# Attention and two gated layers on one core: the band mask added by TensorE in batches 0 and 1, and batch 1's band exponentials cut into 12 ScalarE pieces

## The chip, the cores and the metric

The kernel runs on one core of a Trainium2 chip. The metric is the device time of one execution in microseconds (us). The kernel before took 923.15 us, the median of three runs (922.99 to 925.22). The profiled execution is a run of its own and took 925.11 us.

## The reference, cut to what matters

Attention over 4 batches, 8 heads, 576 positions and 64 columns is computed twice: on positions averaged in fours (144 of them), and on a band in which each position sees only those less than 4 away. Both results are added, and two gated layers follow (512 to 1536 to 512, and 512 to 2048 to 512).

```
mask = np.abs(pos[:, None] - pos[None, :]) < factor          # factor = 4
scores = scale * np.matmul(q, k.transpose(0, 1, 3, 2))
scores = np.where(mask, scores, -1000000000.0)
scores = scores - np.max(scores, axis=-1, keepdims=True)
attn = np.exp(scores)
attn = attn / (np.sum(attn, axis=-1, keepdims=True) + 1e-09)
out_local = np.matmul(attn, v)
return (out_up + out_local).astype(np.float32)
```

The gated layers are `(sigmoid(x @ w_gate) * (x @ w_val)) @ w_out` and `(h * sigmoid(1.702 h)) @ w_out` with `h = x @ w_in`.

## The kernel before, in words

Attention is cut into 16 jobs (`class Job`): four batches, and in each four pairs of heads (`hp`). A job first pools its queries and keys in fours on GpSimd (`pool4`, tiles `half`, `qd`, `kd`). Its band is computed in 24 blocks of 24 queries by 30 keys (`NT`, `NQ`, `NU`): for each block and head one small TensorE matmul writes 32 x 30 scores into a PSUM tile `ss` of 128 partitions, in which the 24 blocks stand as 4 partition quarters by 6 groups (`NG`), for two heads: 2 x 180 columns (`scores`, L668). VectorE then adds the mask into the SBUF tile `sc` (L684), takes the maximum of each group of 30 (L694) and subtracts it (L695); ScalarE exponentiates all 360 columns at once (L697); VectorE sums (L698), inverts (L700), multiplies (L701) and transposes (L702). `band` (L785) multiplies the weights with the values on TensorE. The pooled attention goes beside it: scores (`pooled`, L710), maximum (L727), four exponentials on ScalarE that take the maximum as bias and give the row sum as a second output (L736), the inverse (L743, L744), scaling (L750), transposes (L770), a copy out of PSUM (`pdt`, L775) and the product (L807). The sum of both (`xf`, L820) is split into a high part (`xhi`, L831) and a remainder (`xlo`, L833).

The gated layers multiply in three passes of a high and a low part (L927 to L929); ScalarE makes the high part of each weight (L864) and VectorE the low part (L867). In layer 1 of batch 0 the weights also come as 64-bit words and are converted by ScalarE (L851) and VectorE (L853 to L857). Batch 0's attention has to be done before its layer 1 can begin; the attention of batches 1 to 3 is laid between the matmuls of layer 1 of the batch before. From the second job of batch 1 on, a job is `merged`: band scores and pooled scores share one PSUM tile, `pa`, the only double bank that is left then.

Each engine runs a fixed list of instructions. `class Plan` writes the lists: every operation is registered with `op(engine, nanoseconds, function, reads, writes, due)`, and `order` then places the operations one after another on the engine that is free first, by due time, with the costs that `op` was given. `BEGIN` says when each engine is taken to be free at the start. Where TensorE would be idle in the plan before layer 1 is in full run, fillers are placed: matmuls of the tile `warm` into an unused bank (L1420, 512 or 128 columns). At least one filler stands ahead of each small TensorE operation from 8 us on. A change of an operation or a cost anywhere moves the lists of all engines behind it.

Before the plan begins, `warm` is set to zero by VectorE (L469), GpSimd builds the fp32 mask (L483 to L493) and the fp32 identity `ident` for the transposes.

Of the kernel before, what the change touches and what calls it, by code (L numbers as in the profile page):

```python
# [10 lines left out]
F32 = mybir.dt.float32  # L11
BF16 = mybir.dt.bfloat16
# [3 lines left out]
AF = mybir.ActivationFunctionType  # L16
ALU = mybir.AluOpType
AX = mybir.AxisListType

P = 128  # L20
# [58 lines left out]
class Plan:  # L79
# [12 lines left out]
    MARGIN = 8.0e3  # L92
    WARM_FROM = 8.0e3
    WARM_LEAST = 1
    BEGIN = {"pe": 0.0, "act": 2000.0, "dve": 2200.0, "pool": 3900.0, "sp": 600.0}

    def __init__(self):
        self.ops = []
# [189 lines left out]
def tile_multiscale_attention_gated_ffn(  # L288
# [9 lines left out]
    nc = tc.nc  # L298
    B, NHP, _, S = qT.shape
    D = 64  # L300
# [8 lines left out]
    SCALE = 1.0 / 8.0  # L309
# [13 lines left out]
    NQ, NU = 24, 30  # L323
    NT = S // NQ
    NG = NT // 4
# [3 lines left out]
    sb = ctx.enter_context(tc.tile_pool(name="sb", bufs=1))  # L329
# [5 lines left out]
    op, buf = plan.op, plan.buf  # L335
# [114 lines left out]
    def bank(some):  # L450
        banked.append(Buf(None, some))
        return banked[-1]
# [13 lines left out]

    sb.tile([P, 72], F32, name="inset", tag="inset")
    warm = sb.tile([P, P], BF16, name="warm", tag="warm")
    nc.vector.memset(warm, 0.0)  # L469
    for s in [*qslots, *plan.rings["qt0"][0]]:  # L470
        nc.vector.memset(s.t[:, S:], 0.0)
    for s in [*kslots, *plan.rings["kt0"][0]]:
# [5 lines left out]
    for s in pslots:  # L478
        nc.vector.memset(s.t, 0.0)
        nc.vector.memset(s.t[:, :, :, NU:NU + 1], 1.0e-9)  # L480
    mask = sb.tile([P, NG, NU], F32, name="mask", tag="mask")
    band = plan.rings["xf"][0][0].t[:, :NU]
    nc.gpsimd.memset(band, 0.0)  # L483
    for i in range(4):
# [7 lines left out]
                            fill=NEG, base=-3, channel_multiplier=0)  # L492
    nc.gpsimd.affine_select(out=mask[96:, NG - 1], in_=mask[96:, NG - 1], pattern=[[-1, NU]],  # L493
                            compare_op=ALU.is_ge, fill=NEG, base=S + 2 - NQ * (NT - 1), channel_multiplier=0)
    ident = Buf(Slot(sb.tile([P, P], F32, name="ident", tag="ident")))
    op("pool", 650.0, lambda: make_identity(nc, ident.t), [], [ident], -10.0e3)


    def act_ns(n, psum=False):
        return (126.0 if psum else 190.0) + n / 1.2  # L500

    def dve_ns(n, two=False):
        return 69.0 + n / (1.92 if two else 0.96)
# [1 line left out]
    def pool_ns(n):  # L505
        return 140.0 + 2.12 * n

    def dma(out_, in_, nbytes, reads, writes, due, after=0.0):
        op("sp", nbytes, lambda: nc.sync.dma_start(out=out_, in_=in_), reads, writes, due, after)


    QUANTUM = 3 * 227.0
# [93 lines left out]
    class Job:  # L606
# [49 lines left out]
        def scores(self):  # L656

            ss = bank(self.banks)
            qt, kt, sc, pt, tt, nm, sm = self.qt, self.kt, self.sc, self.pt, self.tt, self.nm, self.sm
            n = NG * NU  # L660

            def scored():
                for t in range(NT):
                    g, i = divmod(t, 4)
                    t = NG * i + g
                    for h in range(2):
                        hs = slice(h * D, (h + 1) * D)
                        nc.tensor.matmul(ss.t[32 * i:32 * i + 32, h, g * NU:(g + 1) * NU],  # L668
                                         qt.t[hs, NQ * t:NQ * t + 32], kt.t[hs, NQ * t:NQ * t + NU],
                                         start=True, stop=True, tile_position=(h * D, 32 * i))  # L670

            when = self.due(0.1)
            if not self.merged:
                op("pe", 1500.0, scored, [qt, kt], [ss, sc], when)
            else:
                qd, kd, nmd, smd, pd = self.qd, self.kd, self.nmd, self.smd, self.pd

                def pe():
                    scored()
                    self.pooled(ss, n)  # L680

                op("pe", 1700.0, pe, [qt, kt, qd, kd],
                   [ss, sc, nmd, (smd, 0), (smd, 1), (pd, 0), (pd, 1)], when)
            op("dve", dve_ns(2 * n), lambda: nc.vector.tensor_add(  # L684
                sc.t.rearrange("p h g c -> p h (g c)"), ss.t[:, :, :n],
                mask.rearrange("p g c -> p (g c)")[:, None, :].to_broadcast([P, 2, n])), [ss], [sc], when)
            if self.merged:
                self.pooled_softmax(ss, n, when, [sc])
# [8 lines left out]
            op("act", act_ns(2 * n), lambda: nc.scalar.activation(p, sc.t, AF.Exp, scale=SCALE), [sc], [pt], at)  # L697
            op("dve", dve_ns(2 * n), lambda: nc.vector.reduce_sum(sm.t, pt.t[:, :, :, :NU + 1], axis=AX.X),  # L698
               [pt], [sm], at)
            op("dve", 155.0, lambda: nc.vector.reciprocal(sm.t, sm.t), [], [sm], at)  # L700
# [765 lines left out]
```

## Time and profile before

| what | value |
|---|---|
| median of three runs | 923.15 us |
| profiled execution | 925.11 us |
| its span | 923.4 us |
| outside the span | 1.7 us |
| TensorE (PE) busy | 909.3 us, 98% of the span |
| VectorE (DVE) busy | 757.0 us, 82% |
| ScalarE (ACT) busy | 508.3 us, 55% |
| GpSimd (POOL) busy | 80.8 us, 9% |

The profile page gives the busy time of each engine over the span. Other views of the trace are used below: busy time and granted TensorE clock by stretch, the waits of an engine, the chain of work that ended last (start, length, engine, tile, line), groups of instructions by line, and the timeline (start, length, engine, line, operation, tiles, shape, count, and the idle time before it with what ended it). Starts are us from the beginning of the span. `pa`, `acc` and `ph` are PSUM banks.

### The profile page before, as it was taken

What the parts mean: (1) busy time and instruction counts of PE and PEld (TensorE: products, weight loads), DVE (VectorE), ACT (ScalarE), POOL (GpSimd) and SP (SyncE); (2) the same over time, 40 slices, a digit from 0 to 9 for tenths busy, and PEclk for the clock granted to TensorE, in tenths of its full rate; (3) what the DMA queues carried; (4) which work ended last, traced back from release to release, by engine and by line L of the source; (5) the groups of instructions that cost most, each with busy time, mean ns of one, the idle gap of its engine ahead of it and who ended that gap; (6) DMA issues with size and microseconds to landing.
All of it is one profiled execution on the core that took longest, in us unless ns stands there. A gap on an engine that the chain in (4) does not pass through costs nothing.

```text
span 923.4 us, 18997 instructions
## 1 busy us (share of the span) xinstructions
PE 909.3 (98%) x7378; PEld 761.8 (83%) x7378; DVE 757.0 (82%) x1432; ACT 508.3 (55%) x1094; POOL 80.8 (9%) x123
## 2 busy tenths in 40 slices
PE   8999999999999999999999999999999999999997
PEld 4677787788888887889999998888888888888896
DVE  4899998988878888899999898878977887765474
ACT  3756664645555555565545655545664553554463
POOL 6211201111011100010000000000301100000000
PEclk8999999999999999999999999999999999999999
DMA  9448548365375834434311651102531100152101
GB/s 287 124 155 229 188 157 244 110 183 174 114 204 185 248 108 135 159 110 141 109 49 42 222 193 46 46 24 84 190 115 69 46 35 34 40 180 78 43 4 23
DMA packets 63949, 113.76 MB, mean 123 GB/s; under 512 B 8241, under 2 KB 29563, under 8 KB 63858
## 3 DMA queue, kind: packets, MB, share of 16 engines
q1 hardware_dynamic: 63858, 112.54, 39.2%
q8 instruction: 58, 0.95, 0.5%
q14 instruction: 33, 0.27, 0.1%
HBM read 82.37 MB, written 30.15 MB: 122 GB/s over the span
## 4 chain that ended last, share of the span: by engine, by line
PE 94%; DVE 2%; POOL 1%; DMA 1%; issue 1%; ACT 1%; POOLq 0%; ACTq 0%
PE ph L927 13%; PE ph L929 13%; PE ph L928 13%; PE acc L927 8%; PE acc L928 8%; PE acc L929 8%; PE pa L927 7%; PE pa L928 7%; PE pa L929 7%; PE pa L785 2%; PE pa L668 1%; PE pa L710 1%; PE pa L770 1%; PE pa L807 1%; PE acc L1420 1%
## 5 line engine op out<-in xcount | busy, mean ns | idle before, releaser
L864 ACT CAST whi<-w 128x512 fp32r<-128x512 f32 x151 | 92.4, 613 | 77.4 <-PE ph L929 28.3
L927 PE MATMUL ph<-xhi,whi 128*128 128x512 f32 (+1 forms) x322 | 127.6, 396 | 0.0
L929 PE MATMUL ph<-xlo,whi 128*128 128x512 f32 (+1 forms) x322 | 124.4, 386 | 0.0
L928 PE MATMUL ph<-xhi,wlo 128*128 128x512 f32 (+1 forms) x322 | 124.4, 386 | 0.0
L867 DVE TENSOR_TENSOR wlo<-w,whi 128x512 fp32r<-128x512 f32 x149 | 103.9, 699 | 17.5 <-ACT whi L864 17.3
L864 ACT CAST whi<-wr 128x512 fp32r<-128x512 f32 (+1 forms) x99 | 55.7, 565 | 35.9 <-PE acc L929 16.5
L867 DVE TENSOR_TENSOR wlo<-wr,whi 128x512 fp32r<-128x512 f32 (+1 forms) x99 | 62.2, 630 | 15.6 <-ACT whi L864 14.7
L927 PE MATMUL acc<-ghi,whi 128*128 128x512 f32 (+1 forms) x192 | 73.7, 384 | 0.0
L927 PEld LDWEIGHTS ph<-xhi,whi 128*128 128x128 f32 x322 | 60.9, 189 | 14.7 <-issue 1.6
L1041 DVE TENSOR_TENSOR w<-pa,w 128x512 f32<-128x512 f32 (+1 forms) x112 | 70.2, 627 | 3.3 <-PE pa L929 2.6
L928 PE MATMUL acc<-ghi,wlo 128*128 128x512 f32 (+1 forms) x192 | 72.4, 377 | 0.4 <-DVE wlo L867 0.4
L929 PE MATMUL acc<-glo,whi 128*128 128x512 f32 (+1 forms) x192 | 72.3, 377 | 0.5 <-DVE glo L867 0.5
L929 PEld LDWEIGHTS ph<-xlo,whi 128*128 128x128 f32 x322 | 60.8, 189 | 12.5
L928 PEld LDWEIGHTS ph<-xhi,wlo 128*128 128x128 f32 x322 | 61.0, 189 | 11.3
L927 PE MATMUL pa<-w,whi 128*128 128x512 f32 (+1 forms) x168 | 61.5, 366 | 0.1
L929 PE MATMUL pa<-w,whi 128*128 128x512 f32 (+1 forms) x168 | 61.4, 366 | 0.0
L928 PE MATMUL pa<-w,wlo 128*128 128x512 f32 (+1 forms) x168 | 61.4, 366 | 0.0
L864 ACT CAST w<-w 128x512 fp32r<-128x512 f32 x51 | 31.1, 619 | 35.7 <-PE pa L929 20.4
L867 DVE TENSOR_TENSOR w<-w,w 128x512 fp32r<-128x512 f32 x48 | 34.3, 721 | 17.0 <-ACT w L864 16.8
L961 ACT ACTIVATE th<-ph 128x512 f32<-128x512 f32 (+1 forms) x44 | 24.6, 559 | 42.8 <-PE ph L929 42.8
L927 PEld LDWEIGHTS acc<-ghi,whi 128*128 128x128 f32 x192 | 36.0, 188 | 7.4 <-issue 1.7
L966 DVE SCALAR_TENSOR_TENSOR th<-th,ph 128x512 f32<-128x512 f32 (+1 forms) x44 | 27.9, 634 | 17.1 <-PE ph L929 12.2
(286 smaller groups left out, 2307.0 us busy)
## 6 DMA issues: line engine op xcount, KB each, us to landing
w<-w SPq DMA_DIRECT2D x68, 512.0 KB
w2d<-we SPq DMA_DIRECT2D x32, 256.0 KB
w<-gd SPq DMA_DIRECT2D x32, 256.0 KB
gd<-w SPq DMA_DIRECT2D x30, 256.0 KB
st<-x2d SPq DMA_DIRECT2D x52, 128.0 KB
w<-w2d SPq DMA_DIRECT2D x16, 256.0 KB
wr<-w2d SPq DMA_DIRECT2D x16, 256.0 KB
out<-ev SPq DMA_DIRECT2D x16, 256.0 KB
```

Of the source, the lines that this page charges most:

```text
L668: nc.tensor.matmul(ss.t[32 * i:32 * i + 32, h, g * NU:(g + 1) * NU], qt.t[hs, NQ * t:NQ * t + 32], kt.t[hs, NQ * t:NQ * t + NU], start=Tru ...
L710: nc.tensor.matmul(ss.t[:GH, h, c + r * G:c + (r + 1) * G], qd.t[h * D:(h + 1) * D, r * GH:(r + 1) * GH], kd.t[h * D:(h + 1) * D, :], star ...
L770: nc.tensor.transpose(ss.t[:GH, h, o:o + GH], pd.t[:, h, r, kh * GH:(kh + 1) * GH], ident.t[:GH, :GH])
L785: nc.tensor.matmul(ss.t[h * D:(h + 1) * D, s, q:q + NQ], vt.t[ks, g, v0 + h * D:v0 + (h + 1) * D], tt.t[ks, h, g, :NQ], start=True, stop=T ...
L864: op("act", act_ns(n), lambda: nc.scalar.copy(vh(), vm()), [rm], [rh], due)
L867: return lambda: on.tensor_sub(vl(), vm(), vh().bitcast(F32))
L927: nc.tensor.matmul(o, lhi, rhi, start=first, stop=False, skip_group_check=more)
L928: nc.tensor.matmul(o, llo, rhi, start=False, stop=False, skip_group_check=more)
L929: nc.tensor.matmul(o, lhi, rlo, start=False, stop=last, skip_group_check=more)
L961: op("act", act_ns(n, True), lambda h=h: nc.scalar.activation(th.t[:, :n], h.t[:, :n], AF.Tanh, scale=0.5 if layer == 1 else 1.702 / 4.0), ...
L966: op("dve", dve_ns(n), lambda: nc.vector.scalar_tensor_tensor(th.t[:, :n], th.t[:, :n], 1.0, hb[-1].t[:, :n], op0=ALU.add, op1=ALU.mult), ...
L1041: op("dve", dve_ns(N), lambda: nc.vector.tensor_add(tmp.t[:, o, :N], b.t[:, :N], tmp.t[:, i, :N]), [b, (tmp, i)], [(tmp, o)], t)
```

## The change

The mask becomes a bf16 tile, and `warm` becomes a bf16 identity that GpSimd builds first; VectorE copies it into the fp32 identity `ident`. In batches 0 and 1, TensorE writes the mask into the score bank with two matmuls `warm` x `mask` of 180 columns, one per head, and the small score matmuls then add onto it. VectorE's addition (L684) is left out there, and the maximum is read from PSUM. In batch 0 the subtraction also reads PSUM and writes `sc`. In batch 1 there is no subtraction: ScalarE scales the maximum by -1/8, and the exponentials are 12 instructions of 30 columns per job (two operations of six), each with the maximum as bias and the row sum as second output; VectorE's sum is left out, and the inverse gets an addition of 1e-9 ahead of it. The plan is told 200 ns more for the scores, 270 ns per piece, and a later begin of VectorE and GpSimd.

```diff
-    BEGIN = {"pe": 0.0, "act": 2000.0, "dve": 2200.0, "pool": 3900.0, "sp": 600.0}
+    BEGIN = {"pe": 0.0, "act": 2000.0, "dve": 4400.0, "pool": 4300.0, "sp": 600.0}
...
-    nc.vector.memset(warm, 0.0)
+    make_identity(nc, warm)
...
-    mask = sb.tile([P, NG, NU], F32, name="mask", tag="mask")
+    mask = sb.tile([P, 2, NG, NU], BF16, name="mask", tag="mask")[:, 0]
...
+    maskb = mask.rearrange("p g c -> p (g c)")
     ident = Buf(Slot(sb.tile([P, P], F32, name="ident", tag="ident")))
-    op("pool", 650.0, lambda: make_identity(nc, ident.t), [], [ident], -10.0e3)
+    nc.vector.tensor_copy(ident.t, warm)
...
+            masked = self.b < 2
+
             def scored():
+                for h in range(2 if masked else 0):
+                    nc.tensor.matmul(ss.t[:, h, :n], warm, maskb, start=True, stop=False, skip_group_check=True)
...
-                                         start=True, stop=True, tile_position=(h * D, 32 * i))
+                                         start=not masked, stop=True, tile_position=(h * D, 32 * i),
+                                         skip_group_check=masked)
...
-            op("dve", dve_ns(2 * n), lambda: nc.vector.tensor_add(
-                sc.t.rearrange("p h g c -> p h (g c)"), ss.t[:, :, :n],
-                mask.rearrange("p g c -> p (g c)")[:, None, :].to_broadcast([P, 2, n])), [ss], [sc], when)
+            x = ss if masked else sc
+            if not masked:
...
-            op("dve", dve_ns(2 * n), lambda: nc.vector.reduce_max(nm.t, sc.t, axis=AX.X), [sc], [nm], at)
-            op("dve", dve_ns(2 * n), lambda: nc.vector.tensor_sub(sc.t, sc.t, spread(nm)), [nm], [sc], at, port=True)
+            op("dve", dve_ns(2 * n), lambda: nc.vector.reduce_max(nm.t, scores_of(), axis=AX.X), [x], [nm], at)
...
+            if self.b == 1:
+                op("act", 200.0, lambda: nc.scalar.mul(nm.t, nm.t, -SCALE), [], [nm], at)
+
+                def grouped(h):
+                    for g in range(NG):
+                        nc.scalar.activation(pt.t[:, h, g, :NU], scores_of()[:, h, g], AF.Exp,
+                                             bias=nm.t[:, h, g:g + 1], scale=SCALE, accum_out=sm.t[:, h, g:g + 1])
+
+                for h in range(2):
+                    op("act", NG * 270.0, lambda h=h: grouped(h), [x, nm], [(pt, h), (sm, h)], at)
+
+                def inverse():
+                    nc.vector.tensor_scalar_add(sm.t, sm.t, 1.0e-9)
+                    nc.vector.reciprocal(sm.t, sm.t)
+
+                op("dve", 250.0, inverse, [], [sm], at)
+            else:
+                op("dve", dve_ns(2 * n), lambda: nc.vector.tensor_sub(sc.t, scores_of(), spread(nm)),
+                   [nm, x] if masked else [nm], [sc], at, port=not masked)
...
```

Behind the `else` stand the old exponential, sum and inverse, unchanged. The lists of all engines are written anew. Three places matter below; line numbers of the change are 1 to 30 higher for the same line (L668 is L673, L743 is L773, L785 is L815).

On TensorE, near the start: the scores and the pooled scores of the first two jobs of batch 0 (`qt_121` and `qt_122`, `qd_132` and `qd_133`). Of the fillers between two operations one row stands for all. Before:

```order
L668 MATMUL pa_159<-kt_123,qt_121 32x30 x48
L1420 MATMUL acc_155<-warm 128x512
L710 MATMUL acc_154<-kd_134,qd_132 72x144 x4
L710 MATMUL pa_159<-kd_135,qd_133 72x144 x4
L668 MATMUL acc_155<-kt_124,qt_122 32x30 x48
L590 MATMUL acc_154<-vt,ones_143 72x256 x12
```

And in the change:

```order
L667 MATMUL pa_159<-mask,warm 128x180
L673 MATMUL pa_159<-kt_123,qt_121 32x30 x48
L740 MATMUL acc_154<-kd_134,qd_132 72x144 x4
L673 MATMUL pa_159<-kt_124,qt_122 32x30 x48
L740 MATMUL acc_155<-kd_135,qd_133 72x144 x4
L591 MATMUL pa_159<-vt,ones_143 72x256 x12
```

The second job's scores moved from behind its pooled scores to ahead of them. Of the fillers, seven stood ahead of the second pooled scores; now three stand ahead of the second scores and one behind them.

On ScalarE, where batch 0 ends: the exponentials of batch 1's first job (L697 before, L709 and L713 now), and `xhi` of the last job of batch 0 (`xf_145`). Before:

```order
L814 ACTIVATE up_142<-acc_154 128x144
L851 ACTIVATE wr_105<-w_86 128x512
L697 ACTIVATE pt_126<-sc_125 128x12x30
L831 CAST xhi_89<-xf_145 128x512
L851 ACTIVATE w_115<-w_86 128x512
L961 ACTIVATE th_97<-ph_149 128x512
```

And in the change:

```order
L709 ACTIVATE small<-small 128x12
L844 ACTIVATE up_142<-acc_154 128x144
L713 ACTIVATE pt_126,small<-pa_159,small 128x30 x12
L861 CAST xhi_89<-xf_145 128x512
L881 ACTIVATE wr_105<-w_86 128x512
```

Twelve pieces stand where one exponential stood, ahead of the last `xhi` of batch 0. The pooled scores of the same job follow on TensorE into the same bank, `pa_159`, so they now wait for ScalarE's pieces.

On VectorE, the softmax of batch 1's last job. Ahead of these rows stand its L684, L694 and L695 before, and its maximum alone in the change. Before:

```order
L743 TENSOR_SCALAR smalld<-smalld 72x4
L744 RECIPROCAL smalld<-smalld 72x4
L966 SCALAR_TENSOR_TENSOR th_97<-th_97,ph_149 128x512
L698 TENSOR_REDUCE small<-pt_127 128x12
L853 TENSOR_SCALAR w_119<-w_119 128x512
L700 RECIPROCAL small<-small 128x12
L855 SCALAR_TENSOR_TENSOR w_119<-w_86,w_119 128x512
L701 TENSOR_TENSOR pt_127<-pt_127,small 128x12x30
L970 TENSOR_TENSOR glo_95<-th_97,ghi_93 128x512
L702 STREAM_TRANSPOSE tt_129<-pt_127 128x384
```

And in the change:

```order
L773 TENSOR_SCALAR smalld<-smalld 72x4
L774 RECIPROCAL smalld<-smalld 72x4
L887 SCALAR_TENSOR_TENSOR w_112<-w_86,w_112 128x512
L996 SCALAR_TENSOR_TENSOR th_97<-th_97,ph_150 128x512
L897 TENSOR_TENSOR wlo_84<-w_112,whi_80 128x512
L720 TENSOR_SCALAR small<-small 128x12
L721 RECIPROCAL small<-small 128x12
L731 TENSOR_TENSOR pt_127<-pt_127,small 128x12x30
L1000 TENSOR_TENSOR glo_95<-th_97,ghi_93 128x512
L732 STREAM_TRANSPOSE tt_129<-pt_127 128x384
```

From the job's first operation to its transpose VectorE had 20 instructions and now has 12. On TensorE, 36 matmuls of layer 1 stood between this job's scores and its band product; now there are 96, and the third job's band product and transposes besides. One job's transposes (L770, now L800) are followed directly by its band and its product with the values, which wait for ScalarE's copy: the first job's before, the third's now.

## Rows read from the trace of the kernel before

**Rows 1.** The page: busy us (share of the span) x instructions.
```profile
PE 909.3 (98%) x7378; PEld 761.8 (83%) x7378; DVE 757.0 (82%) x1432; ACT 508.3 (55%) x1094; POOL 80.8 (9%) x123
```
**Rows 2.** Busy time by stretch: length, engines (x instructions), granted clock, DMA share, GB/s.
```profile
13.03:60.16 47.13, 46.10 (x998) 31.86 (x998) 37.61 (x72) 30.06 (x81) 14.35 (x19) 0.93 0.60 193
60.16:200.00 139.84, 137.60 (x1503) 110.64 (x1503) 129.87 (x233) 83.03 (x187) 17.55 (x20) 0.99 0.62 179
```
**Rows 3.** Waits of TensorE, whole span: total us, times, longest us.
```profile
PE pa L710 <- POOL kd L638: 3.4, 1, 3.4
PE pa L785 <- DVE tt L702: 1.1, 1, 1.1
PE pa L785 <- ACT pdt L775: 0.7, 1, 0.7
PE acc L928 <- DVE wlo L867: 0.4, 1, 0.4
```
**Rows 4.** Timeline of TensorE, 7 to 14 us.
```profile
7.94 1.69 PE L1420 MATMUL acc<-warm 128*128 128x512 bf16 x7
13.03 1.24 PE L710 MATMUL pa<-kd,qd 64*72 64x144 f32 x8 [3.41 <-POOL kd L638]
```
**Rows 5.** The chain that ended last, 13 to 25 us: start, length, what.
```profile
14.27 0.54 PE acc L1420
14.81 1.15 PE acc L668 x74
...
16.50 4.10 PE acc L590 x24
20.60 0.32 PE acc L1420
...
21.64 2.74 PE pa L590 x24
```
**Rows 6.** TensorE by stretches of 1 us: length, busy, granted clock, DMA share, GB/s.
```profile
18.00:19.00 1.00, 1.00 (x6) 0.50 1.00 397
19.00:20.00 1.00, 1.00 (x10) 0.89 1.05 410
```
**Rows 7.** Groups of VectorE by line and shape: busy us, mean ns, idle before.
```profile
L695 DVE TENSOR_TENSOR sc<-sc,small 128x360 f32<-128x360 f32 x16 | 8.6, 540 | 0.3
L698 DVE TENSOR_REDUCE small<-pt 128x12 f32<-128x372 f32 x16 | 8.3, 518 | 5.5 <-ACT pt L697 5.4
L684 DVE TENSOR_TENSOR sc<-pa,mask 128x360 f32<-128x360 f32 x13 | 6.8, 526 | 3.7 <-POOL ones L1367 3.3 <-PE pa L710 0.4
```
**Rows 8.** Timeline of ScalarE, 9 to 27 us.
```profile
9.19 0.38 ACT L736 ACTIVATE pd<-acc,smalld 72x144 f32<-72x144 f32 x1
9.47 0.19 ACT L736 ACTIVATION_READ_ACCUMULATOR pd<-acc,smalld 72x1 f32 x1
9.56 0.36 ACT L736 ACTIVATE pd<-acc,smalld 72x144 f32<-72x144 f32 x1
...
9.91 0.49 ACT L697 ACTIVATE pt<-sc 128x360 f32<-128x360 f32 x1
...
20.68 0.58 ACT L594 COPY vd<-acc 72x512 f32<-72x512 f32 x1 [3.79 <-PE acc L590]
...
26.22 0.29 ACT L814 ACTIVATE up<-acc 128x144 f32<-128x144 f32 x1 [0.64 <-PE acc L807]
```
**Rows 9.** The chain that ended last, 128 to 146 us.
```profile
128.63 0.23 PE ph L928
...
130.73 0.53 DVE sc L684
...
139.56 0.50 DVE tt L702
```
**Rows 10.** Timeline of TensorE, 138 to 146 us.
```profile
142.06 0.59 PE L929 MATMUL ph<-xlo,whi 128*128 128x512 f32 x1
...
145.44 0.43 PE L928 MATMUL ph<-xhi,wlo 128*128 128x512 f32 x1
```

More of the change, by code (lines that the diff above doesn't have):

```diff
@@ L506, in pool_ns, with dma @@
         return 140.0 + 2.12 * n
-    def dma(out_, in_, nbytes, reads, writes, due, after=0.0):
-        op("sp", nbytes, lambda: nc.sync.dma_start(out=out_, in_=in_), reads, writes, due, after)
+    def dma(out_, in_, nmaskeds, reads, writes, due, after=0.0):
+        op("sp", nmaskeds, lambda: nc.sync.dma_start(out=out_, in_=in_), reads, writes, due, after)
     QUANTUM = 3 * 227.0
@@ L669, in scored @@
                                          qt.t[hs, NQ * t:NQ * t + 32], kt.t[hs, NQ * t:NQ * t + NU],
-                                         start=True, stop=True, tile_position=(h * D, 32 * i))
+                                         start=not masked, stop=True, tile_position=(h * D, 32 * i),
+                                         skip_group_check=masked)
             when = self.due(0.1)
             if not self.merged:
-                op("pe", 1500.0, scored, [qt, kt], [ss, sc], when)
+                op("pe", 1500.0 + 200.0 * masked, scored, [qt, kt], [ss, sc], when)
             else:
@@ L680, in pe @@
                     self.pooled(ss, n)
-                op("pe", 1700.0, pe, [qt, kt, qd, kd],
+                op("pe", 1700.0 + 200.0 * masked, pe, [qt, kt, qd, kd],
                    [ss, sc, nmd, (smd, 0), (smd, 1), (pd, 0), (pd, 1)], when)
-            op("dve", dve_ns(2 * n), lambda: nc.vector.tensor_add(
-                sc.t.rearrange("p h g c -> p h (g c)"), ss.t[:, :, :n],
-                mask.rearrange("p g c -> p (g c)")[:, None, :].to_broadcast([P, 2, n])), [ss], [sc], when)
+            x = ss if masked else sc
+            if not masked:
+                op("dve", dve_ns(2 * n), lambda: nc.vector.tensor_add(
+                    sc.t.rearrange("p h g c -> p h (g c)"), ss.t[:, :, :n],
+                    mask.rearrange("p g c -> p (g c)")[:, None, :].to_broadcast([P, 2, n])), [ss], [sc], when)
             if self.merged:
-                self.pooled_softmax(ss, n, when, [sc])
+                self.pooled_softmax(ss, n, when, [x])
             def spread(x):
@@ L693, in scores, with scores_of @@
             at = self.due(0.15)
-            op("dve", dve_ns(2 * n), lambda: nc.vector.reduce_max(nm.t, sc.t, axis=AX.X), [sc], [nm], at)
-            op("dve", dve_ns(2 * n), lambda: nc.vector.tensor_sub(sc.t, sc.t, spread(nm)), [nm], [sc], at, port=True)
+            def scores_of():
+                return ss.t[:, :, :n].rearrange("p h (g c) -> p h g c", c=NU) if masked else sc.t
+            op("dve", dve_ns(2 * n), lambda: nc.vector.reduce_max(nm.t, scores_of(), axis=AX.X), [x], [nm], at)
             p = pt.t[:, :, :, :NU]
[L697 to L700, printed above, removed]
+            if self.b == 1:
[13 more added lines that the diff above has]
+                   [nm, x] if masked else [nm], [sc], at, port=not masked)
+                op("act", act_ns(2 * n), lambda: nc.scalar.activation(p, sc.t, AF.Exp, scale=SCALE), [sc], [pt], at)
+                op("dve", dve_ns(2 * n), lambda: nc.vector.reduce_sum(sm.t, pt.t[:, :, :, :NU + 1], axis=AX.X),
+                   [pt], [sm], at)
+                op("dve", 155.0, lambda: nc.vector.reciprocal(sm.t, sm.t), [], [sm], at)
             op("dve", dve_ns(2 * n), lambda: nc.vector.tensor_mul(p, p, spread(sm)), [sm], [pt], at, port=True)
```

## The prediction

> **What bounds the kernel now.** I read the page first: TensorE is busy for 98% of the span, VectorE for 82%, ScalarE for 55% [rows 1]. So time can come only from three things: less work on TensorE, shorter waits of TensorE, or a higher clock. The busy time by stretch shows where another engine has a say: from 60 to 200 us, beside the attention of batch 1 and part of batch 2, VectorE is busy for 129.9 of 139.8 us (93%) and ScalarE for 59% [rows 2]. From 13.03 to 60.16 us, up to the first result product of layer 1, TensorE is at it for 46.10 of 47.13 us, but fillers are part of that [rows 2]. The waits of TensorE are few: 3.4 us for the pooled keys of the second job, 1.1 us for a transpose of the band's weights, 0.7 us for a copy of ScalarE, 0.4 us for a low part [rows 3]. The granted clock is 2.4 GHz nearly throughout. It was halved to 1.2 GHz twice: around 13 to 19 us, after the 3.41 us wait [rows 4, 6], and around 142 to 145 us, after the 1.1 us wait [rows 3, 10].
>
> The profiled execution took 925.11 us, 1.96 us above the median of 923.15. The second halving alone is worth 1.5 us: from 142.06 to 145.44 there are eight spaces, 3.38 us, where eight at 0.23 us would be 1.84 [rows 9, 10]. I take it, without having it shown, that the median runs lack it.
>
> **The change part by part.** *VectorE.* Eight additions of 0.53 us go, four each in batches 0 and 1 [rows 7]. In batch 1 the subtraction (0.54) and the sum (0.52) go too [rows 7], and a small addition of under 0.2 us comes: 1.4 us less per job there, 0.53 in batch 0. On an engine that is 93% busy this shortens the chain from scores to transposed weights. The reads that move from `sc` to PSUM I price at nothing: L684 reads PSUM and takes 0.53 us, L695 reads SBUF and takes 0.54 [rows 7].
>
> *The start.* The identity moves from behind the mask to the head of GpSimd's list: the same two instructions, so the pooled keys are ready as before, and the fillers begin a few tenths later. TensorE waits for 3.41 us there [rows 4], which covers that. The gain is in what moves into this wait. Behind the second job's pooled scores stood its band scores (1.15 us) and a filler (0.54 us) [rows 5]; both are now ahead of it. From there to the first result product the two lists otherwise differ by two small fillers more (a full-clock filler of 512 columns is 0.32 us [rows 5], so 0.08 each) and three pairs of mask matmuls. One of these has 180 columns: 180/512 of 0.32 us is 0.11, a pair 0.22. Lower bound 0.16 by 0.23 us per 512 columns [rows 9]; upper bound 0.5, if each mask matmul cost as much as the 0.23 us of a whole one. Sum: -1.15 - 0.54 + 0.16 + 0.67 = **-0.86 us**.
>
> *The new wait.* The pooled scores of batch 1's first job go into the bank from which ScalarE now reads 12 pieces; the last `xhi` of batch 0 stands behind the pieces, too. What is a piece? An exponential of 144 columns with bias and second output begins at 9.19, its readout at 9.47, the next exponential at 9.56: 0.37 us in all [rows 8]. Between 144 and 512 columns ScalarE's PSUM reads differ by 0.29 us [rows 8], 0.79 ns a column, so 114 columns fewer save 0.09: **0.28 us** a piece, 3.4 us for twelve, where one exponential took 0.49 [rows 8]. The Trainium skill ("ScalarE: Activation LUTs", the rules for kernel authors) says to budget about 0.3 us for each ACTIVATE with a per-partition bias, plus 0.83 ns a column, which speaks against cutting one into twelve. By that budget, with the readout of 0.09 us on top, a piece would be an estimated 0.42 us; the case is among the rivals. The plan was told 0.27 us, so its lists leave room for 0.28, but not for what VectorE and ScalarE are behind at that point. The bounds of the wait are 0 (the fillers, four and more, cover it) and 2.9 us (3.4 - 0.49, all uncovered). I take **+0.8 us**, near the 0.7 us wait for a copy by ScalarE [rows 3], which also stands behind other work in its list.
>
> *Batch 1's three merged jobs.* Three more pairs of mask matmuls on a TensorE without slack: 3 x 0.22 = **+0.67 us** (bounds 0.5 to 1.5). ScalarE gets 2.9 us more per job; at 59% busy I take that as hidden, with 0.7 us, one more wait of the kind in [rows 3], as the upper bound.
>
> *The stalls beside batch 1.* The chain runs through VectorE from 130.73 to 140.06 us [rows 9]: the last job's 20 instructions take 9.3 us, and 36 matmuls at 0.23 us [rows 9] cover only 8.3; hence the wait of 1.1 us [rows 3]. Now 12 instructions stand there, three fifths, some 5.6 us, with 3.4 us of pieces beside or between them, against 96 matmuls, 22 us. The stall goes: **-1.1 us**. The wait of 0.4 us for a low part comes from the same full VectorE; I take it as gone: **-0.4 us**, bound 0. The wait of 0.7 us stays, since one job's transposes are still followed directly by what waits for their copy: 0.
>
> Sum: -0.86 + 0.8 + 0.67 - 1.1 - 0.4 = **-0.9 us**. Against the profiled 925.11, where the halving after the stall goes as well (-1.5), that is 922.7; against the median, 922.3. I forecast **922.4 us**, between them.
>
> **The rivals.** *The pieces are dearer.* If fewer columns save nothing, a piece is 0.37 us [rows 8], 0.09 more than I took; 48 pieces make 4.3 us. ScalarE hands out the high parts in list order, and the plan was told 0.27, so in four jobs TensorE could wait for nearly all of it: 922.4 + 4.3 = 926.7 us. If ScalarE's 41% of idle time covers half, it is 924.6. The case decides for slower from about 0.36 us a piece, 0.08 more, if nothing covers it. For it: pieces stand in front of `xhi` and of high parts. Against it: a copy of 144 columns already takes only half of one of 512 [rows 8]. By the Trainium skill's budget in the section named above the estimate would be 48 x 0.14 = 6.7 us more, 929; the overlap in [rows 8], where the next instruction begins 0.09 us before the last has ended, speaks against that. Chance 0.10.
>
> *The first halving shrinks.* TensorE's wait before the second job's pooled scores shortens from 3.4 us to about 2.3: fillers and scores end about 1.1 us later (scores 1.0, two mask pairs 0.4, later fillers 0.4, one filler 0.3, four fillers fewer -0.9). Behind this wait TensorE ran at 1.2 GHz and was back at 2.4 GHz only after 19 us [rows 6]. In that stretch a group of value sums took 4.10 us, and its twin at full clock 2.74 [rows 5]. With a shorter halving this 1.4 us comes back, 921.0; with none, the pooled scores' and two fillers' excess (0.5 and 0.4) also, and 920.1. The Trainium skill ("TensorE: Matmul & The Clock Gate", the clock-gate part) has the clock follow how busy the array has been, so that a shorter idle stretch may leave it up. The trace has a fall even after 1.1 us of waiting [rows 3, 10], so I give this 0.23.
>
> *No gain.* The end of the start is set by VectorE and ScalarE, not by TensorE's list: the pieces in front of the last `xhi` then cost up to 2.9 us while the scores moved forward buy nothing but more filler time: 923.3 to 925.2. For it: fillers stand up to 53 us. Chance 0.13.
>
> **How the numbers follow.** My forecast's own case, 921.1 to 923.8 by its bounds, has 0.54. 0.3% is 2.8 us here, about what a measurement can tell from no change: faster means below 920.4, slower above 925.9. Faster needs the second rival, in full or in part with the mask matmuls and the new wait at their lower bounds: 0.18 of its 0.23. Slower: the dear pieces with little cover, 0.07 of 0.10, and 0.03 of the no-gain case, where other waits come on top. Same: 0.72. The range of 919.6 to 925.6 takes in the first rival's lower half, all of the third, and the second with its bounds.
>
> **What would show it.** Right: groups of 12 pieces 0.28 us apart; pairs of mask matmuls of about 0.2 us; the second job's scores ahead of 13 us; a wait of TensorE of a microsecond or less for the pieces near 50 us; the first result product near 60 us; no wait for L732 near 139 us and full clock behind it. Wrong: pieces 0.36 us or more apart; several waits of TensorE for ScalarE between 60 and 200 us; a first result product later than 61 us; a new stall with a halved clock behind it.

## The result and the profile after

The change made the kernel slower: 930.67 us median of 4 runs (928.46 to 931.74) against 923.68 us for the kernel before (median of 4), a ratio of 1.0075 with a 95% interval of 1.0057 to 1.0092. The forecast was 922.4 us, with 925.6 us as the upper end. The profiled execution took 930.1 us, its span is 928.4 us with a mean granted clock of 0.988; before, 923.4 us and 0.993.

The page and the busy time by stretch of the changed kernel, in the same stretches as [rows 1, 2]:

```profile
PE 912.7 (98%) x7392; PEld 764.9 (82%) x7392; DVE 749.3 (81%) x1421; ACT 517.0 (56%) x1190; POOL 84.8 (9%) x122
```

```profile
13.03:60.16 47.13, 42.94 (x883) 28.80 (x883) 31.55 (x59) 28.95 (x99) 15.22 (x15) 0.83 0.57 180
60.16:200.00 139.84, 138.24 (x1478) 111.62 (x1477) 125.09 (x228) 91.72 (x260) 17.36 (x20) 0.99 0.62 178
```

The engines are about as busy as before; the stretch up to 60.16 us is not. Its granted clock fell from 0.93 to 0.83, and TensorE began 883 matmuls there instead of 998. Which waits are behind that, the waits of TensorE show (total us, times, longest), beside [rows 3]:

```profile
PE acc L740 <- issue: 6.7, 2, 4.8
PE acc L1450 <- POOL xf L483: 1.4, 1, 1.4
PE pa L667 <- ACT pt L713: 0.9, 1, 0.9
PE pa L815 <- ACT pdt L805: 0.7, 1, 0.7
PE acc L959 <- DVE glo L897: 0.4, 1, 0.4
```

The wait for the pooled keys is no longer named. In its place stand two stops of 6.7 us in all, put down to "issue": TensorE waited for nothing that the profile shows. The timeline of TensorE has their places:

```profile
10.12 0.39 PE L1450 MATMUL acc<-warm 128*128 128x512 bf16 x1
15.29 1.24 PE L740 MATMUL acc<-kd,qd 64*72 64x144 f32 x8 [4.78 <-issue]
...
21.23 0.39 PE L1450 MATMUL acc<-warm 128*128 128x512 bf16 x1
...
36.46 0.46 PE L740 MATMUL acc<-kd,qd 64*72 64x144 f32 x2
38.85 0.65 PE L740 MATMUL acc<-kd,qd 64*72 64x144 f32 x6 [1.93 <-issue]
...
45.67 0.63 PE L958 MATMUL ph<-xhi,wlo 128*128 128x512 f32 x1
...
65.76 0.58 PE L957 MATMUL acc<-ghi,whi 128*128 128x512 f32 x1
```

Part of the first stop is still the wait for the keys. GpSimd's timeline has the second job's pooled keys ready at 12.36 us:

```profile
11.94 0.42 POOL L639 TENSOR_TENSOR kd<-half 128x144 f32<-128x144 f32 x1
```

So of the 4.78 us up to 15.29 TensorE would have waited 1.9 us for them in any case; 2.9 us have no operand behind them.

The second stop is the telling one: it stands inside one operation, between the second and the third of eight records with the same operands. Behind it the clock was at half for ten microseconds (length, busy by engine, granted clock, DMA share, GB/s):

```profile
38.00:40.00 2.00, 1.15 (x12) 0.60 (x15) 0.39 (x1) 0.00 (x0) 0.22 (x1) 0.91 0.94 213
40.00:42.00 2.00, 2.00 (x54) 1.94 (x56) 1.90 (x5) 1.03 (x5) 0.00 (x0) 0.50 0.24 60
...
46.00:48.00 2.00, 2.00 (x6) 1.17 (x6) 1.97 (x7) 1.82 (x6) 1.13 (x1) 0.50 0.28 92
48.00:50.00 2.00, 2.00 (x101) 1.38 (x99) 1.92 (x3) 1.17 (x3) 1.69 (x1) 0.53 0.00 0
```

The first result product (the first L957 into `acc`) begins at 65.76 us instead of 60.16: all of the 5.0 us by which the span grew, and 0.6 more. From there to the end it is 862.6 us now and was 863.2.

**What a stop for "issue" is.** Counted from the start of the span, TensorE had begun this many matmuls and weight loads when it stopped, in the changed kernel first at 10.5 us and then at 36.9 (window; then busy (x instructions) of TensorE's matmuls and of its weight loads, and the other engines):

```profile
0.00:15.00 15.00, 9.07 (x222) 4.90 (x223) 7.69 (x32) 5.26 (x16) 9.65 (x39) 0.91 0.90 240
0.00:38.00 38.00, 30.70 (x731) 18.97 (x732) 22.68 (x60) 19.44 (x58) 21.84 (x53) 0.91 0.75 228
```

The kernel before has one such stop as well, of 0.73 us. It stands in the list of waits beside those of [rows 3], and in the timeline again within one operation; its count follows:

```profile
PE pa L785 <- issue: 0.7, 1, 0.7
```

```profile
33.86 0.41 PE L785 MATMUL pa<-tt,vt 30*64 30x24 f32 x12 [0.73 <-issue]
```

```profile
0.00:33.50 33.50, 28.66 (x604) 17.03 (x605) 18.94 (x53) 15.31 (x44) 17.78 (x50) 0.90 0.77 234
```

222, 604 and 731 matmuls: 604 is 222 and three times 127 (and one), 731 is 604 and 127. With as many weight loads, the stops lie a multiple of some 255 instructions apart. The page's part on DMA queues has a queue named for it (packets, MB, share of 16 engines):

```profile
q8 instruction: 58, 0.95, 0.4%
```

58 packets of 16 KB for TensorE's 14,784 matmuls and weight loads are 255 each. In the changed kernel packets of this queue begin at 12.70 and 35.59 us, 2.6 and 3.3 us before the two stops end. Ahead of the second stop TensorE had begun the 127 matmuls since the boundary before in 3.0 us (33.65 to 36.64 us), and the packet at 35.59 is the only one in that time. So my theory A: TensorE gets its instructions in blocks, and where it runs through one faster than the next arrives, it stops. A small fp32 matmul (L673, L740, L815) shows as two matmuls and two weight loads; the 96 records of one job's scores take 1 us and three quarters of a block. The Trainium skill ("Runtime: NRT & Kernel Launch", section "Instruction fetch mechanics") has this picture, blocks of 16 KiB or 256 instructions that the sequencer fetches by a DMA queue of its own, and says that crossing a boundary is mostly hidden. The counts agree with the block; the stops of 4.78 and 1.93 us disagree with "hidden".

### The profile page after: what moved, and what is told of

It is laid out like the page before. It is cut to its first block, busy times and chain, and to the rows that moved or that the text cites. A ratio compares the mean times of both kernels' runs of the same rounds, so it can differ in the third digit from the quotient of the medians.

```text
span 928.4 us, 19106 instructions
## 1 busy us (share of the span) xinstructions
PE 912.7 (98%) x7392; PEld 764.9 (82%) x7392; DVE 749.3 (81%) x1421; ACT 517.0 (56%) x1190; POOL 84.8 (9%) x122
## 4 chain that ended last, share of the span: by engine, by line
PE 93%; DMA 2%; DVE 2%; ACT 1%; issue 1%; POOL 1%; POOLq 0%; SPq 0%; DVEq 0%; ACTq 0%
PE ph L957 13%; PE ph L959 13%; PE ph L958 12%; PE acc L957 8%; PE acc L959 8%; PE acc L958 8%; PE pa L957 7%; PE pa L958 7%; PE pa L959 7%; PE pa L815 2%; DMA w<-w 2%; PE pa L673 1%; PE pa L837 1%; PE pa L800 1%; PE acc L1450 1%
## 5 line engine op out<-in xcount | busy, mean ns | idle before, releaser
L957 PE MATMUL ph<-xhi,whi 128*128 128x512 f32 (+1 forms) x322 | 127.7, 397 | 0.0
L957 PE MATMUL acc<-ghi,whi 128*128 128x512 f32 (+1 forms) x192 | 73.8, 384 | 0.0
L957 PEld LDWEIGHTS ph<-xhi,whi 128*128 128x128 f32 x322 | 61.1, 190 | 14.7 <-issue 2.0
L957 PE MATMUL pa<-w,whi 128*128 128x512 f32 (+1 forms) x168 | 61.5, 366 | 0.1
L957 PEld LDWEIGHTS acc<-ghi,whi 128*128 128x128 f32 x192 | 36.0, 188 | 7.2 <-issue 1.5
```

Source lines behind the costliest of these rows:

```text
L957: nc.tensor.matmul(o, lhi, rhi, start=first, stop=False, skip_group_check=more)
```

## The experiments

Rivals: **B**, ScalarE's pieces and the masks themselves cost the time; **C**, the second pooled scores wait for an operand; **D**, the clock falls because the matmuls are small, stop or no stop. Medians of the kernel before, taken on the same chip beside each group of runs, were 924.1 to 924.5 us (923.7 beside the change itself). Nothing computed changes unless it is said.

### The parts alone, and the place of the stop

Masks without pieces, pieces without masks, both in batch 1 alone:

```diff
-            if self.b == 1:                 # e1: softmax with pieces
+            if False:
-            masked = self.b < 2             # e2; e3: masked = self.b == 1
+            masked = False
```

> The mask by TensorE in batches 0 and 1 as in the change, but batch 1 keeps the subtraction, the single exponential and the sum. TensorE's list at the start is that of the change: the second job's band scores stand ahead of its pooled scores. Theory A (TensorE waits for its own instructions: in the changed kernel it stops at its 444th and 1463rd instruction, with no data missing, and restarts 2.6 to 3.3 us after a 16 KB packet on its instruction queue began): the stop of 4 to 5 us near 15.3 us stays, the first result product comes at about 65.5 us, and the time is 928 to 931 us. Rival B (ScalarE's pieces delay the start and the steady part): with no pieces the first result product is back near 60.5 us and the time 921 to 924 us.

> Batch 1's exponentials in 12 pieces as in the change, but the mask is added by VectorE in all batches. TensorE's list at the start is that of the kernel before. Theory A (waits for TensorE's own instructions): the block of instructions has come while TensorE waits for the second job's pooled keys, so no stop of more than 1 us beyond that wait; the first result product at 60 to 61.5 us, 922 to 925 us in all. Rival B (the pieces cost it): 926 to 930 us, with waits of TensorE for ScalarE in the stretch from 50 to 200 us.

> Both parts of the change in batch 1 alone; batch 0's mask is added by VectorE as before. TensorE's list at the start is that of the kernel before. Theory A: first result product at 60 to 61.5 us and the better steady part of the changed kernel (0.6 us less behind the first result product), 921.5 to 924 us. Rival B: slower than the kernel before by 3 us or more, for the pieces and batch 1's masks are all there.

Measured: masks alone 926.50 us (ratio 1.0026, 1.0012 to 1.0040), pieces alone 930.68 us (1.0063, 1.0046 to 1.0080), batch 1 alone 927.70 us (1.0037, 1.0021 to 1.0054). Neither theory had it. Masks alone kept the stop of 5.1 us as A said, but came out at 926.5; pieces alone had a stop of only 0.9 us and were as slow as the whole change, as B said. The order of the lists changes with every part, so a part alone is not a part alone; for pieces alone and for batch 1 alone the expectations took TensorE's list at the start to be that of the kernel before, and it was not. In batch 1 alone the planner moved a third job's scores forward, and a stop of 2.15 us with a halved clock behind it came at 36 us, at 731 matmuls again.

The whole change, with the first 12 fillers each split into four of 128 columns: the same columns, 36 matmuls and as many weight loads more.

```diff
+        if o in small and split < 12:
+            split += 1
+            for _ in range(4):
+                small[o].fn()
+            continue
         o.fn()
```

> The whole change; the first 12 fillers of 512 columns are each given as four of 128, so the same columns in 72 more TensorE instructions ahead of the first stop. Theory A: the stop follows the count of instructions, not the operation: it moves from the second job's pooled scores into the middle of the second job's band scores, about 60 of their 96 matmul records in, and again ends near 15.3 us, with 929 to 932 us in all. Rival C (the second job's pooled scores wait for their operand, their bank or a transfer): the band scores run through and the same pooled scores start late again.

Measured: 929.41 us (1.0046, 1.0019 to 1.0072). The timeline of TensorE in this kernel at its two stops, and the counts at both:

```profile
15.54 0.55 PE L673 MATMUL pa<-kt,qt 64*32 64x30 f32 x35 [4.86 <-issue]
...
48.24 0.21 PE L673 MATMUL pa<-kt,qt 64*32 64x30 f32 x1 [2.91 <-issue]
```

```profile
0.00:15.00 15.00, 9.25 (x222) 7.91 (x223) 6.19 (x28) 3.54 (x11) 10.36 (x41) 0.98 0.91 253
0.00:47.00 47.00, 38.89 (x987) 27.69 (x987) 30.45 (x75) 25.58 (x77) 24.68 (x54) 0.93 0.69 208
```

The first stop left the pooled scores and stands in the band scores, 61 records in and 35 to go, where A put it; C is out. The count is 222 again, and the second stop went on to 987, 256 behind 731. The first stop ends at 15.3 to 16.2 us in every kernel that had one: the block comes then, whichever operation stands there.

### The order held fixed

Here the planner was made to give TensorE the kernel before's order at the start: GpSimd's begin 200 to 250 ns later, and where batch 0 is masked, the second job's scores behind its pooled scores.

```diff
-    BEGIN = {..., "pool": 4300.0, ...}
+    BEGIN = {..., "pool": 4550.0, ...}
-                op("pe", 1500.0 + 200.0 * masked, scored, [qt, kt], [ss, sc], when)
+                op("pe", 1500.0 + 200.0 * masked, scored, [qt, kt] + ([self.kd] if (self.b, self.hp) == (0, 1) else []), [ss, sc], when)
-            at = self.due(0.5)
+            at = self.due(0.05 if (self.b, self.hp) == (0, 1) else 0.5)
```

> Neither masks by TensorE nor pieces: of the change only the identity at the head of GpSimd's list and the planner's two start numbers that go with it. That alone gives TensorE another order after the first job: a third job's scores from 21 us on, the second group of value sums some 8 us later (as in the runs with pieces alone and with batch 1 alone). Theory A (the order at the start decides when TensorE reaches the end of the instructions that it has, and the clock halves behind the longer of these stops): a stop of 1 to 2.5 us near 37 us, the first result product at 62 to 66 us, 925.5 to 929 us in all. Rival B (pieces and masks cost the time): like the kernel before, 923 to 925 us.

> Both parts in batch 1 alone, and the planner's start number of GpSimd 200 ns later, which gives TensorE the order of the kernel before at the start. Theory A: stop near 33 us of about 0.7 us as before, first result product at 60 to 61 us, 921.5 to 924 us. Rival B: 927 to 928 us as with the other order, for the same pieces and masks are in it.

> The whole change, masks in batches 0 and 1 and pieces in batch 1; the second job's scores are planned behind its pooled scores, so TensorE's order of operations at the start is that of the kernel before (with the mask matmuls in front of the scores). Theory A: no stop of 4.8 us near 15 us and none of 1.9 us near 38 us; the first result product at 60.5 to 62 us; 922 to 925 us. Rival B: 929 to 931 us as the change.

> Pieces in batch 1, mask by VectorE everywhere, with the kernel before's order on TensorE at the start. Theory A: 923 to 926 us, 5 to 7 us less than the same pieces with the other order. Rival B: 929 to 931 us, as with the other order.

Measured: neither part, with the order that the planner gives it, 924.38 us (1.0016, 1.0003 to 1.0029; a stop of 0.6 us, first result product at 61.7): A missed, that order alone costs next to nothing. Batch 1 alone 926.30 us (1.0025, 1.0007 to 1.0043), between A and B. The whole change 926.93 us (1.0024, 1.0005 to 1.0042), 3.7 us less than the change, by order alone, but not the 922 to 925 of A. Pieces alone 924.34 us (1.0012, 1.0000 to 1.0025), 6.3 us less than the same pieces with the other order. So the order is a large part, and something is left in the parts. Then the masks without pieces, and neither, in that same order:

```diff
-            if self.b == 1:                 # e13; e14: masked = self.b == 1 too
+            if False:
-            masked = self.b < 2             # e15: with both lines
+            masked = False
```

> Masks by TensorE in batches 0 and 1, no pieces, and TensorE's order at the start as in the kernel before. If the order at the start and the pieces are the whole loss: first result product at 60.5 to 62.5 us, the remainder 859 to 861 us (the stall near 139 us gone), 921 to 924 us. If the masks themselves cost time: 925 us or more.

> The mask by TensorE in batch 1 alone, no pieces, order at the start as in the kernel before. If the masks relieve VectorE beside batch 1: the stall of 1.1 us near 139 us and the halved clock behind it gone, 920.5 to 923.5 us. If the four mask pairs on TensorE (0.9 us) eat that: 923.5 to 925 us.

> Neither masks nor pieces: only the identity's move, and the order at the start as in the kernel before. Both theories: like the kernel before within 1 us, 923.5 to 925 us. Against it the run with pieces and the same order (924.3 us) prices the pieces alone: 0.5 to 2 us less here if ScalarE's pieces delay TensorE, 1 us more here if relieving VectorE in batch 1 pays.

Measured: masks in both batches 922.81 us (0.9985, 0.9973 to 0.9996), in batch 1 alone 923.04 us (0.9984, 0.9969 to 0.9999), neither 925.07 us (1.0002, 0.9992 to 1.0012). **The masks without pieces, in the old order, come out some 1.4 us (0.15%) below the kernel before**, with intervals that end just short of no difference. With masks in both batches the first result product came at 63.34 us, later than expected, but the expectation on the remainder held: 63.34 to 922.5 are 859.2 us, 4.1 less than before. With the masks in place the four cells add up:

| masks in batches 0 and 1 | order of before | order of the change | difference |
|---|---|---|---|
| without pieces | 922.81 | 926.50 | 3.7 |
| with pieces | 926.93 | 930.67 | 3.7 |
| difference | 4.1 | 4.2 | |

The masks gain 1.5 us; the order takes 3.7 and the pieces 4.1. By the ratios to the kernel before the four differences are 3.6 to 4.7 us, and by the intervals each is uncertain by some 2 us. The profiles show where the pieces cost it: from the first result product to the end the two kernels with pieces take 862.6 and 863.1 us, the two without 858.9 and 859.2. They don't show the same for the order: the profiled runs of the masks without pieces happen to be equally long in both orders (924.21 and 924.25 us, first result product at 63.56 and 63.34), so its 3.7 us rest on the medians.

With the mask on VectorE this does not hold. In the old order pieces cost nothing that stands out of the noise: 924.34 against 925.07 us by the medians, 0.9 us more by the ratios. In the other order they cost 6.3 us by the medians (930.68 less 924.38), 4.3 by the ratios.

### What the stops and the clock are worth

Fillers more at one place, by repeating one that the plan has there: in the change 12 behind 33.9 us; the same and 20 ahead of the second job's scores; in the kernel before 14 in its first wait; and these with one more in each of 12 gaps.

```diff
     for o in plan.order():
         o.fn()
+        if o in whole and last not in whole:
+            for _ in range(more.get(groups, 0)):
+                o.fn()
+            groups += 1
+        last = o
```

> The whole change, with 12 fillers of 512 columns more (2.8 us of work that computes nothing) some 2.5 us ahead of the place near 37 us where TensorE stopped for 1.93 us and after which the clock was halved from 39 to 49 us. Theory A (the stop brings the clock down, and the halved clock is most of the loss): the stop shrinks under 0.5 us, no halved clock between 20 and 60 us, the first result product comes 2 to 4 us earlier than in the changed kernel, at 62 to 64 us, and the time falls to 926 to 928.5 us although work was added. Rival D (the clock falls because the matmuls there are small, with or without a stop): still halved near 39 us, 931 to 934 us.

> As the run before, and 20 fillers more ahead of the second job's scores, where the changed kernel stopped for 4.78 us up to 15.3 us. Theory A: that stop shrinks to under 1 us, the clock is not halved from 12 to 20 us either, the first group of value sums takes 2.8 to 3 us instead of 3.45, first result product at 60 to 62 us, 922 to 926 us in all. Rival D: halved clock as in the changed kernel, 931 to 937 us.

> The kernel before, without any part of the change, with 14 fillers more in the 3.41 us in which TensorE waits for the second job's pooled keys. Theory A: no halving from 12 to 19 us; the first group of value sums takes 2.8 instead of 4.10 us; 1.5 to 3 us less than the kernel before, 920.5 to 923 us. Rival D (small matmuls bring the clock down anyway): no gain, 923.5 to 925 us.

> The kernel before with 14 fillers in its first wait, and one full filler more in each of 12 gaps between the groups of small matmuls of batch 0 (2.8 us of added work). If the clock falls there because little of the array is in use: no halved clock between 12 and 60 us, the first result product at 58 to 60.5 us against 61.7 us with the first wait alone filled, 921 to 923.5 us. If it falls regardless: halved for 10 us or more again, first result product at 63 to 65 us, 925.5 to 928 us.

With the second stop filled: 928.61 us (1.0047, 1.0029 to 1.0064), **2.1 us less than the change although 2.8 us of work was added**, just above A's range and well below D's. The second stop is gone (the first, 5.09 us up to 16.21, is still there), and the same operations as above run at full clock:

```profile
35.08 2.98 PE L1450 MATMUL acc<-warm 128*128 128x512 bf16 x13
...
40.43 0.71 PE L740 MATMUL acc<-kd,qd 64*72 64x144 f32 x8
...
64.17 0.58 PE L957 MATMUL acc<-ghi,whi 128*128 128x512 f32 x1
```

From the end of the first group of value sums to the first result product it is 22.32 to 64.17, 41.85 us here with the fillers in it; in the change 21.23 to 65.76, 44.53 us; before 20.53 to 60.16, 39.63 us. Stop and halved clock are worth the 5.4 us by which 44.53 exceeds 41.85 less 2.76. (The fillers also make the work there denser, so whether the clock stayed up for that or for the missing stop is not separated.) A stop of 0.95 us came at 97.8 us instead, at 1,496 matmuls, ten blocks behind the first.

With both stops filled: 929.73 us (1.0059, 1.0036 to 1.0082). A missed. In the profiled run, the fastest of the four, the clock was good (a mean of 0.998; the others had 0.990 to 0.994), but 1.07 us of the stop at 222 matmuls were left and 0.93 us came at the next boundary, 349 (timeline, and the counts):

```profile
16.14 0.31 PE L673 MATMUL pa<-kt,qt 64*32 64x30 f32 x19 [1.07 <-issue]
...
23.68 0.52 PE L673 MATMUL pa<-w,w 64*32 64x30 f32 x36 [0.93 <-issue]
```

```profile
0.00:15.50 15.50, 13.63 (x222) 6.63 (x223) 6.26 (x28) 3.54 (x11) 9.90 (x40) 1.00 0.91 235
0.00:23.00 23.00, 20.25 (x349) 10.70 (x349) 10.53 (x39) 8.20 (x28) 14.18 (x47) 1.00 0.94 286
```

The kernel before with its first wait filled: 924.65 us (1.0002, 0.9987 to 1.0017), no gain, as D said. The first group of value sums took 2.82 us instead of 4.17, but at 26 us the clock fell all the same, with no stop ahead of it, amid small matmuls with a single filler between groups:

```profile
24.00:26.00 2.00, 2.00 (x59) 1.43 (x57) 1.29 (x3) 1.42 (x4) 0.00 (x0) 0.93 0.00 0
26.00:30.00 4.00, 4.00 (x152) 3.23 (x153) 3.90 (x7) 1.70 (x3) 1.90 (x2) 0.50 0.73 224
```

That is the profiled run, with a mean clock of 0.991. Eight of the ten runs of this kernel had 0.995 to 0.999, which leaves no room for the 13 us at half that this one has from 26 us on, and they took 922.6 to 925.6 us. So the fall at 26 us does not explain why a filled wait gained nothing; that stays open.

With two fillers between those groups (927.98 us; 1.0034, 1.0022 to 1.0045; no gain either) the clock stayed at full up to 36 us, until a stop of 2.33 us came, at 732 matmuls, and fell right behind it:

```profile
34.00:36.00 2.00, 0.79 (x92) 0.67 (x68) 1.39 (x4) 1.35 (x5) 1.13 (x1) 1.00 0.50 142
36.00:38.00 2.00, 0.89 (x6) 0.32 (x6) 0.52 (x1) 0.00 (x0) 1.19 (x3) 0.50 0.41 115
```

So both are seen in these profiles: the clock falls behind a stop, and it can fall amid small matmuls without one. A last try filled the one remaining stop of 1.32 us in the best version (six fillers):

> Masks by TensorE, no pieces, order of the kernel before at the start, and 6 fillers of 512 columns more (1.4 us) just ahead of the place where TensorE stopped for 1.32 us near 34 us and had a halved clock for 3.4 us behind it. Theory A (stop, then halved clock): stop under 0.3 us, no halved clock from 20 to 60 us, 1 to 2 us less than without the fillers (922.8 us): 921 to 922 us. If the clock falls there without a stop too, or nothing was lost: 922.5 to 924.5 us.

Measured: 923.99 us (0.9995, 0.9983 to 1.0007), a miss. In the profiled run the stop there and the halved clock behind it are gone, but 0.92 us of stop came at the next boundary (731 matmuls), and the fillers are 1.4 us of work themselves; whether that is all of it is not shown.

### What the pieces are worth

Each piece issued twice (pieces alone, old order):

```diff
-                    for g in range(NG):
+                    for g in [g for g in range(NG) for _ in range(2)]:
```

> The pieces with the order of the kernel before on TensorE (mask by VectorE), but every piece is issued twice, so 24 where the change has 12: about 3.1 us more of ScalarE for each of the four jobs of batch 1. If ScalarE's time for pieces is covered by other work: within 1.5 us of the same kernel with single pieces (924.3 us). If pieces are on the path of TensorE: 927.5 to 936 us, with waits of TensorE for the exponentials.

Measured: 950.55 us (1.0280, 1.0259 to 1.0302), 26 us more and beyond both cases of the expectation, where ScalarE is busy for 19.1 us more by the two pages (519.8 and 538.9 us; 0.40 us for each of the 48 pieces added, more than the expectation had). The waits of TensorE name the buffers that ScalarE fills late:

```profile
PE ph L957 <- ACT xhi L861: 5.2, 1, 5.2
PE ph L957 <- ACT whi L894: 4.5, 1, 4.5
...
PE pa L815 <- ACT pdt L805: 3.0, 2, 1.8
PE pa L815 <- ACT up L844: 1.9, 1, 1.9
```

None of these waits names the pieces themselves; they are for work that stands behind the pieces in ScalarE's list. The rest is the clock: a mean of 0.979 over 949.9 us is 40 us at half clock, against 0.995 over 922.3 us, 9 us, with single pieces. 30 us more at half clock is about 15 us lost, which leaves some 12 of the 27.6 us between the spans: by this estimate well over half of ScalarE's 19.1 us was covered by nothing.

In the change the pieces are as cheap as forecast. The group by line (ns, minimum/median/maximum; first and last start), and two starts in ScalarE's timeline:

```profile
L713 ACT ACTIVATE pt<-pa,small x48: 267/296/352, 54.1 to 140.6; 128x30 f32<-128x30 f32 x48
L713 ACT ACTIVATION_READ_ACCUMULATOR pt<-pa,small x48: 190/218/275, 54.3 to 140.8; 128x1 f32 x48
```

```profile
54.10 0.28 ACT L713 ACTIVATE pt<-pa,small 128x30 f32<-128x30 f32 x1
...
54.36 0.29 ACT L713 ACTIVATE pt<-pa,small 128x30 f32<-128x30 f32 x1
```

Where they cost it is seen near 142 us. TensorE's timeline in the change, and then in the masks without pieces:

```profile
142.18 0.89 PE L815 MATMUL pa<-tt,vt 30*64 30x24 f32 x48
143.00 0.69 PE L800 MATMUL pa<-ident,pd 72*72 72x72 f32 x8
144.42 0.89 PE L815 MATMUL pa<-tt,vt 30*64 30x24 f32 x48 [0.72 <-ACT pdt L805]
```

```profile
142.11 0.89 PE L815 MATMUL pa<-tt,vt 30*64 30x24 f32 x48
142.93 0.69 PE L800 MATMUL pa<-ident,pd 72*72 72x72 f32 x8
151.78 0.89 PE L815 MATMUL pa<-tt,vt 30*64 30x24 f32 x48
```

Without pieces, result products stand between the groups and cover ScalarE's copy. With them, the groups fall together, TensorE waits for the copy, and the clock is halved at 146 us (six spaces with 0.2 to 0.36 us over their 0.23, and 0.35 us more for L837: 1.7 us). Together with the 0.87 us for which the mask matmuls at 121 us wait for the last piece to leave `pa`, the only bank that batch 1's scores have, this is some 3.3 us of the 4. That the bank, held by the pieces, explains why they are free where VectorE copies the scores out of it (-0.7 us) was not tried by itself.

## Why the prediction was wrong

- **The start, forecast -0.86 us, measured about +5.6.** This is the step that failed: "The gain is in what moves into this wait." The wait of 3.41 us for the pooled keys [rows 3, 4] was read as one wait with one releaser. It covered a second arrival: in every kernel that stopped there, the block with the 223rd matmul came no sooner than at 15.3 us; in the kernel before TensorE, held up by the keys, got to that matmul at 15.6. Scores moved forward only brought it there at 10.5 us. The first group of value sums ended 0.7 us later instead of earlier. Of the other 4.9 us, 1.2 are the longer second stop (1.93 against 0.73), and most of the rest, some 3.5 us (5.4 less the stop of 1.93), the ten microseconds at half clock behind it. The runs with fillers show that part; those with the order held fixed give 3.7 us by their medians for the order as a whole. A stop of the same kind, 0.73 us, stood in the list of waits of the kernel before; the prediction named four waits and not this one.
- **The rival of the first halving** read the wait the same way: it did not shrink, and a second one came. "A new stall with a halved clock behind it" stood among the signs of an error, without a mechanism or a chance.
- **The new wait at `pa_159`, forecast +0.8 us near 50 us**: not there, but at 121 us, 0.87 us.
- **Mask pairs, forecast 0.22 us**: 0.25 us in the timeline (34.22 to 34.47). Right.
- **Pieces, forecast 0.28 us each**: 0.26 us from start to start with the readout. Right; from SBUF, in the run with pieces alone, it is 0.31 us. The Trainium skill's budget ("ScalarE: Activation LUTs", the rules for kernel authors), by which the forecast had estimated 0.42 us, was too high for both. But "at 59% busy I take that as hidden" is the second step that failed, put at nothing: with the masks by TensorE the pieces cost 4.1 us in either order, behind the first result product; with the masks by VectorE and the order of before, none that can be told from noise.
- **The stalls beside batch 1, forecast -1.5 us**: both gone, and the halved clock behind the first with them; another came at 146 us, behind the wait for ScalarE's copy. Without pieces the 0.7 us for ScalarE's copy, forecast to stay, goes as well, and the remainder is 4.1 us shorter; in the change only 0.6.
- **Dear pieces**, the rival on the slow side, gave 924.6 to 926.7 us: its sign held, its cause did not.

## What to carry to other kernels

A wait in a profile names the releaser that came last. Before work is moved ahead of it, ask what else arrives during it, TensorE's own instructions among them: count the matmuls and weight loads up to each "issue" stop, and see how fast many small fp32 matmuls use up a block. When a scheduler rewrites the order with each part of a change, hold the order fixed before a part is priced; here about half the loss was the order, and one part in the old order was a small gain. An engine at 60% busy may still be on the path: issuing its new work twice shows it at once.

## What had not been expected of the hardware

Each of the 33 stops for "issue" in the profiles of these 19 kernels fell at 222, 349, 604, 731 or 732, 859, 986 or 987, or 1,496 matmuls, whatever operation stood there: steps of 127 or 128, or a multiple. They were 0.2 to 5.1 us long. After stops of 1.3 us and more on the way to the first result product the clock was at half in every profile; after 0.4 to 1.1 us in some and not in others. What decides that is open. Runs of one kernel spread by up to 10 us, and the mean granted clock goes with it: within the kernels, 0.001 less of it came with about 0.7 us more (correlation -0.80 over the 155 runs of the 18 other kernels).
